# A hedgehog-attention and token-shift-MLP block: value products of the first three tiles in column halves, and a new order of the lists

## The chip, the cores and the metric

The kernel runs on one core of one Trainium2 chip. The metric is the device time of one execution in microseconds (us), the median of several runs. Engine names are those of the profile: PE is TensorE's matmul, PEld its weight load, DVE is VectorE, ACT is ScalarE, POOL is GpSimd, and SP is SyncE, which here only issues DMAs. A bank is one of the 8 banks of 2 KB per partition in PSUM, into which matmuls write.

## The reference

One block with two branches on x of 2048 tokens by 448 channels in bf16. H is 16 heads of 28 channels.

```
xn = layernorm(x)
# A: linear attention
q, k, v = split(xn @ wqkv)                      # 16 heads of 28
phi(u)  = [softmax(u @ w_phi), softmax(-(u @ w_phi))]
kv = phi(k)^T v ;  z = sum_s phi(k)
A  = (phi(q) kv / (phi(q) z + 1e-6)) @ wo
# B: token-shift MLP
h  = gelu(layernorm(xn) @ w1)                   # 448 -> 448
hs = four groups of 112 channels, shifted by +1, -1, +2, -2 tokens, @ w2
x1 = xn + hs
B  = x1 + gelu(layernorm(x1) @ w3) @ w4         # 448 -> 1792 -> 448
y  = x + A + B
```

## The kernel before

The tokens are 16 tiles of 128. Everything stays in SBUF: `xtok` (x), `xn` (normalized), `xnT` (its transpose, channels on partitions), `vaug` (the values with a column of ones per head), `phik` (features of the keys), `g_tok`/`gT` (the normalized x1 and its transpose), `hT` (the output of the first MLP).

**Two row halves.** A product over 448 channels is split into matmuls that use 64 rows of the PE array each. The lower and the upper 64 rows work at the same time, each into a bank of its own, so each product comes as a pair of lists. A value product of one tile (`z_v`, called ZV in the head's list) is 7 matmuls of 448 columns with the tile's `xnT` as weights and `wv` as the moving operand; a product with w1 (ZW) is 7 matmuls of 512 columns, and ZH is half of one, 7 matmuls of 256 columns. Transposes on TensorE (XT: `xn_T`, evacuated by `xn_out`) are 8 matmuls of 64x64 by an identity for each tile.

**Recorder.** All instructions are recorded in program order, and each engine executes its own in that order; semaphores are worked out from what they read and write. The line numbers in the profile are mostly those of the recorder's helpers: L204 is every matmul, L208 every transpose on TensorE, L212 an ACT instruction, L216 an elementwise instruction of DVE or POOL, L222 a DMA, L219 a DMA transpose. L737 is the product of the features of the keys with their normalizer on POOL.

**The loads** are issued by SP and ACT at the start, in the order in which they stand (`load_x(i, n)` loads n tiles from tile i, `load_half` half of a weight).

**The head** is a list given to `chain`. Its entries are executed in order. L entries are steps of the layernorm: "m" is statistics of a tile on DVE (bn_stats and bn_aggr), "q" its reciprocal root on ACT, "r" the same on POOL, "a" the application on DVE, "p" on POOL, "s" and "t" the statistics and root of tile 1 on ACT. XT are transposes, XD transposes by DMA, HD matmuls on constants that keep TensorE busy, FO the folding of `w_phi` into the weights of q and k, ZR the last 64 columns of the products with w1, HF the first pairs of the stage that follows. EV and EW are the evacuations of a value product and of a w1 product. "zip" jobs are interleaved between the two row halves by `chain` with a lag of 400 columns and a string of digits that says which half gets the next job first. `vb` and `gb` name the banks of the value products and of the w1 products.

**The rest** is a list given to `play`, executed in order. k0/k1 and q0/q1 are the products and exponentials of the key and query features, w0/w1_ the products with w2, kn and kx the normalizers and the products (POOL, L737) of the key features, lo and sc the statistics of the second layernorm, A and AD its application on POOL and DVE into `g_tok`, G its transpose by DMA into `gT` (issued by SP), K the products kv of a tile (matmuls of 64 columns on `phik` and `vaug`), a and b the products with w3 (512 columns on `gT`) and w4's input, T the transpose of the query features, N, f and S the output with its divisions and stores. `load_w4(h)` loads one of the two halves of w4, 784 KB, on SP; SP issues its DMAs in the list's order, and a DMA that waits for its data holds back all behind it.

Of the kernel before, what the change touches and what calls it, by code (L numbers as in the profile page):

```python
# [224 lines left out]
def bass_parallel_sum__linear_kernel_hedgehog__mixer_s_mlp__prompt_kernel(  # L225
    nc, A_x, A_wqkv, A_w_phi, A_wo, B_x, B_w1, B_w2, B_w3, B_w4, out,
):
    _, S, D = A_x.shape
# [14 lines left out]
    with es:  # L243
# [106 lines left out]
        def load_x(i, n, eng="SP"):  # L350
            R.dma(xtok[:, i:i + n, :], x2d[128 * i:128 * (i + n), :].rearrange("(j p) d -> p j d", p=128), eng)
# [9 lines left out]
        def load_half(dst, src, h, eng="SP"):  # L361
            R.dma(dst[:, 2 * h:2 * h + 2, :], src[192 * h:192 * h + 256, :].rearrange("(c p) d -> p c d", p=128), eng)
# [568 lines left out]
        def ZW(g, m, *then):  # L931
            return "zip", z_w1(g, m, gb[g][m]), then
# [21 lines left out]
        def HF(p, n):  # L954
# [4 lines left out]
        vb = {0: 5, 1: 6, 2: 5, 3: 0, 4: 7, 5: 5, 6: 0, 7: 1, 8: 0, 9: 6, 10: 3, 11: 2, 12: 7, 13: 7, 14: 5, 15: 2}  # L959
        gb = ((4, 2, 3), (7, 6, 4), (5, 0, 7), (0, 5, 6))  # L960
        spin(30)
        chain([
            L(("m", 0)), L(("s", 1, 0)), L(("q", 0, 1)), L(("s", 1, 1)), L(("a", 0)), HD(3, 3), L(("t", 1)), HD(0, 3),
            HD(1, 3), L(("p", 1)), L(("m", 2)), HD(5, 3), L(("q", 2, 1)), L(("m", 3)), do(load_w2, 0), HD(0, 3),
            HD(0, 3), XT(0, 5, 1, "2"), L(("m", 4)), L(("p", 2)), L(("q", 3, 1)), XT(1, 0, 1, "ACT"),
            ZV(0, EV(0, "ACT", 1)), XT(2, 0, 1, "ACT"), ZV(1, EV(1, "ACT", 1)), L(("q", 4, 1)), L(("m", 5)),
            L(("a", 4)), L(("p", 3)), ZH(2, 0), L(("q", 5, 1)), inside(1, ZH(1, 0), XT(3, 0, 1, "ACT")), L(("m", 7)),
            L(("q", 7, 1)), L(("m", 6)), L(("a", 7)), do(load_wT, 0, (1, 2, 3)), ZV(2, EV(2, "ACT", 1)),
            inside(1, ZH(0, 0), XT(4, 0, 1, "ACT")), L(("p", 5)),
            inside(2, ZH(0, 1, EW(0, 0, 1)), XT(5, 6, 1, "DVE")), L(("q", 6, 1)), L(("p", 6)), L(("m", 14)),  # L970
            L(("m", 15)), inside(1, ZH(2, 1), XT(7, 0, 1, "ACT")), ZV(4, EV(4, "ACT", 1)),
            inside(2, ZH(1, 1, EW(0, 1, 2)), XT(6, 0, 1, "DVE")), ZV(5, EV(5, "ACT", 1)), L(("r", 14, 1)),
            L(("r", 15, 1)), ZV(6, EV(6, "ACT", 1)), L(("m", 13)), ZW(1, 1, EW(1, 1, 1)), ZW(1, 2, EW(1, 2, 1)),
            L(("a", 14)), L(("a", 15)), L(("m", 12)), L(("m", 10)), XT(14, 1, 2, "2"), L(("r", 12, 1)),
            ZW(1, 0, EW(1, 0, 1)), L(("m", 11)), L(("m", 8)), L(("p", 12)), ZV(3, EV(3, "ACT", 1)), L(("r", 13, 1)),
            L(("a", 13)), L(("r", 10, 1)), ZV(7, EV(7, "DVE", 1)), L(("r", 8, 1)), L(("p", 8)),
            ZV(15, EV(15, "ACT", 1)), L(("a", 10)), XT(12, 6, 1, "2"), XD(10), XT(13, 3, 1, "DVE"),
            ZV(14, EV(14, "ACT", 1)), ZV(12, EV(12, "ACT", 1)), do(phi_blocks), L(("m", 9)), ZW(3, 0, EW(3, 0, 1)),
            L(("r", 11, 1)), XT(8, 1, 1, "2"), FO(1, 0, 0), L(("p", 11)), L(("r", 9, 1)), L(("p", 9)),
            ZW(3, 2, EW(3, 2, 1)), XD(11), FO(1, 0, 1), FO(1, 2, 0), ZW(3, 1, EW(3, 1, 1)), FO(1, 2, 1),  # L980
            do(load_w2, 1), ZV(13, EV(13, "ACT", 1)), ZV(8, EV(8, "DVE", 1)),
            inside(3, ZR(0, 6, (rest_out, 0, 6), (rest_T, 0)), XT(9, 1, 1, "DVE")), FO(0, 0, 0), FO(0, 2, 0),
            do(h_shift, 0), ZW(2, 2, EW(2, 2, 1)), ZW(2, 1, EW(2, 1, 1)), FO(0, 0, 1), ZW(2, 0, EW(2, 0, 1)),
            do(late_3), FO(0, 2, 1), ZV(9, EV(9, "DVE", 1)), do(kv_picks), ZR(1, 7, (rest_out, 1, 7)),
            ZV(10, EV(10, "DVE", 1)), ZV(11, EV(11, "DVE", 1)), HF(1, 0), HF(0, 0), HF(2, 0), do(load_w3, 0),
            do(kv_ones), do(h_shift, 1), do(rest_T, 1), HF(1, 1), HF(0, 1), HF(2, 1)], 400,
            "101001101001101000100110011110100")
# [62 lines left out]
        def wo_in(eng="SP"):  # L1050
# [1 line left out]

        K, G, S, T, kc, kb, W = kv_tile, g_T, store, q_T, kv_turn, kv_blocks, fin_tails
        play([
            (lo, 1), (load_w3, 1), (k0, 1), (w0, 2), (lo, 0), (kn, 0), (k1, 1), (q0, 1), (w1_, 2), (q1, 1), (T, 0),
            (k0, 2), (q0, 2), (k1, 2), (q1, 2), (k0, 3), (q0, 3), (T, 1), (kn, 1), (T, 3), (k1, 3), (w0, 4), (q1, 3),
            (kx, 0), (kn, 2), (T, 2), (kx, 1), (w1_, 4), (kn, 3), (k0, 4), (T, 5), (w0, 6), (k1, 4), (lo, 3), (kx, 2),
            (q0, 4), (lo, 2), (w1_, 6), (q1, 4), (kn, 4), (k0, 5), (kx, 3), (k0, 6), (sc, 0), (k1, 5), (w0, 8),
            (wo_in,), (q0, 5), (A, 0), (w1_, 8), (k1, 6), (T, 6), (AD, 1), (T, 4), (q0, 6), (kn, 5), (T, 7), (q1, 5),
            (w0, 10), (load_w4, 0), (A, 3), (k0, 7), (A, 2), (w1_, 10), (q1, 6), (lo, 5), (lo, 6), (w0, 12), (k1, 7),  # L1060
            (q0, 7), (G, 0), (K, 0), (kx, 4), (K, 1), (G, 1), (kx, 5), (lo, 7), (lo, 4), (G, 2), (K, 3), (K, 4),
            (G, 3), (sc, 4), (K, 6), (A, 7), (kn, 6), (K, 9), (q1, 7), (load_w4, 1), (A, 6), (A, 4), (w1_, 12),
            (K, 8), (K, 5), (K, 7), (lo, 10), (A, 5), (K, 11), (K, 2), (kx, 6), (G, 4), (kn, 7), (G, 7), (K, 10),
            (a, 0), (lo, 11), (kx, 7), (a, 1), (G, 6), (b, 0), (lo, 12), (b, 1), (w0, 14), (a, 2), (lo, 8), (a, 3),
            (lo, 9), (b, 2), (G, 5), (b, 3), (sc, 8), (w1_, 14), (T, 15), (a, 4), (a, 5), (b, 4), (b, 5), (T, 12),
            (lo, 14), (K, 13), (lo, 15), (T, 10), (K, 15), (K, 14), (T, 14), (K, 12), (a, 6), (a, 7), (A, 9), (b, 6),
            (G, 9), (b, 7), (kc,), (kb,), (T, 9), (A, 11), (AD, 10), (N, 1), (T, 11), (f, 1, 0), (N, 0), (a, 9),
            (AD, 8), (a, 8), (b, 9), (b, 8), (G, 10), (N, 2), (f, 2, 0), (a, 10), (G, 11), (lo, 13), (sc, 12),
            (A, 15), (a, 11), (N, 3), (b, 10), (G, 8), (f, 3, 0), (AD, 13), (A, 14), (b, 11), (f, 4, 0), (N, 5),
            (T, 13), (T, 8), (a, 12), (a, 13), (b, 12), (f, 1, 1), (b, 13), (S, 1), (A, 12), (N, 4), (f, 2, 1),  # L1070
            (N, 7), (a, 14), (f, 3, 1), (a, 15), (f, 4, 1), (b, 14), (G, 12), (S, 2), (b, 15), (S, 0), (N, 9),
            (G, 15), (f, 1, 2), (a, 16), (a, 17), (N, 6), (b, 16), (b, 17), (f, 2, 2), (G, 13), (N, 8), (a, 18),
            (f, 3, 2), (b, 18), (f, 4, 2), (a, 19), (N, 11), (a, 20), (G, 14), (S, 3), (f, 1, 3), (f, 3, 3), (N, 13),
            (b, 20), (b, 19), (f, 2, 3), (S, 5), (f, 4, 3), (a, 21), (N, 10), (a, 22), (S, 7), (b, 21), (f, 1, 4),
            (f, 3, 4), (S, 4), (b, 22), (N, 15), (f, 2, 4), (a, 23), (f, 4, 4), (S, 6), (a, 24), (b, 23), (f, 1, 5),
            (N, 12), (b, 24), (f, 2, 5), (N, 14), (a, 25), (S, 9), (S, 8), (f, 3, 5), (b, 25), (f, 4, 5), (a, 26),
            (a, 27), (b, 26), (b, 27), (f, 1, 6), (S, 10), (f, 2, 6), (fin_tails,), (f, 3, 6), (S, 12), (S, 13),
            (S, 11)])
        fin_full(14)
        fin_out(14)  # L1080
        store(14)
# [31 lines left out]
```

## Time and profile before

| | |
|---|---|
| median of 3 runs | 170.38 us (170.35 to 171.14) |
| the profiled execution's own time | 171.91 us |
| its span | 170.2 us |
| granted TensorE clock | 1.00 |
| PE busy | 164.4 us, 97% of the span, 2355 matmuls |
| DVE, POOL, ACT busy | 110.2, 91.0, 80.1 us |
| DMA | 19.93 MB, mean 117 GB/s |

A matmul's row gives its partitions and the columns that it streams ("64*128 64x448": 64 rows of weights 128 wide, 448 columns). "Busy" is the time in which the engine ran at least one of the instructions of a group, so overlapping matmuls count once, and the mean of one is longer than busy time over count. The chain of waits lists what the end of the execution hung on, piece by piece; "issue" in it is time in which an engine waited for nothing that the profile shows. In the table of DMA queues, "instruction" marks packets that carry instructions to the engines.

### The profile page before, as it was taken

To read this page: it belongs to the slowest core of one execution; us is meant where nothing else is said; L and a number is where in the kernel's file an instruction comes from. 1 tells how busy PE (TensorE), PEld (TensorE's weight loads), DVE (VectorE), ACT (ScalarE), POOL (GpSimd) and SP (SyncE) were. 2 spreads that over 40 slices of the span, in tenths; PEclk is the share of its full clock that TensorE was granted. 3 is DMA by queue.
4 is the path that set the end of the run, shared out by engine and by line. 5 is a ranking of instruction groups with operands and counts; after the bars stand their busy time and mean duration, and the time that the engine had idled before them with its cause. 6 is when DMAs were issued, how large, how long until landed. Compare 5 with 4: busy or idle time off the path is not lost.

```text
span 170.2 us, 5418 instructions
## 1 busy us (share of the span) xinstructions
PE 164.4 (97%) x2355; PEld 100.7 (59%) x2355; DVE 110.2 (65%) x249; ACT 80.1 (47%) x110; POOL 91.0 (53%) x124
## 2 busy tenths in 40 slices
PE   8699999999999999899999999999999999999994
PEld 7476778766888875444555455545555555545453
DVE  3679975669999999993785836745754252570031
ACT  4689775649998787445342430430240222224000
POOL 5633994002999999994365693162362634252040
PEclk9999999999999999999999999999999999999999
DMA  4996544988999966549885149363233112014021
GB/s 123 339 230 107 135 94 105 180 211 246 194 132 239 231 97 192 62 90 134 170 99 105 34 98 181 64 117 52 43 66 85 32 57 62 0 31 113 3 81 54
DMA packets 50553, 19.93 MB, mean 117 GB/s; under 512 B 41698, under 2 KB 49826, under 8 KB 50530
## 3 DMA queue, kind: packets, MB, share of 16 engines
q1 hardware_dynamic: 49410, 18.71, 54.2%
q10 hardware_dynamic: 1120, 0.89, 1.6%
q8 instruction: 18, 0.29, 0.8%
q14 instruction: 5, 0.04, 0.1%
HBM read 7.14 MB, written 1.84 MB: 53 GB/s over the span
## 4 chain that ended last, share of the span: by engine, by line
PE 90%; DMA 5%; SPq 2%; DVE 1%; issue 1%
PE banks L204 89%; DMA xtok<-in_A_x_dram 5%; SPq L222 2%; DVE st L216 1%; PE banks L208 0%; DVE mv L216 0%; DVE xnT L216 0%; DVE vaug L216 0%
## 5 line engine op out<-in xcount | busy, mean ns | idle before, releaser
L212 ACT ACTIVATE phik<-banks 128x1024 bf16<-128x1024 f32 (+1 forms) x44 | 41.7, 988 | 64.1 <-PE banks L204 64.0
L204 PE MATMUL banks<-gT,w 64*128 64x512 bf16 x392 | 47.3, 376 | 0.6 <-issue 0.5
L216 DVE TENSOR_TENSOR vaug<-banks,vaug 128x464 f32<-128x464 f32 (+3 forms) x65 | 32.8, 514 | 20.6 <-PE banks L204 18.8
L204 PE MATMUL banks<-w,phik 64*128 64x448 bf16 (+3 forms) x434 | 45.2, 343 | 0.0
L216 POOL TENSOR_TENSOR xnT<-vaug 128x280 bf16<-128x280 f32 (+1 forms) x32 | 18.1, 587 | 35.9 <-DVE vaug L216 35.9
L204 PEld LDWEIGHTS banks<-w,phik 64*128 64x128 bf16 (+1 forms) x434 | 22.3, 94 | 19.5 <-issue 0.4
L737 POOL TENSOR_TENSOR phik<-phik,rks 128x1792 bf16<-128x1792 bf16 x8 | 25.6, 3211 | 14.7 <-DVE rks L216 14.7
L204 PE MATMUL banks<-wv,xnT 64*128 64x448 bf16 (+2 forms) x222 | 32.1, 346 | 0.9 <-DMA wv<-in_A_wqkv_dram 0.6
L204 PEld LDWEIGHTS banks<-gT,w 64*128 64x128 bf16 x392 | 18.3, 94 | 20.1 <-ACT phik L212 1.2
L216 POOL TENSOR_TENSOR vaug<-xn,xtok 128x448 f32<-128x448 bf16 x16 | 16.2, 1031 | 9.1 <-DVE vaug L216 9.1
L204 PEld LDWEIGHTS banks<-wv,xnT 64*128 64x128 bf16 (+1 forms) x222 | 14.1, 94 | 9.4 <-DVE xnT L216 0.9
L216 DVE RECIPROCAL vaug<-banks 128x16 f32<-128x16 f32 x16 | 4.1, 257 | 22.0 <-PE banks L204 22.0
L204 PE MATMUL banks<-xnT,w 64*128 64x512 bf16 (+1 forms) x105 | 16.6, 334 | 0.1
L216 DVE TENSOR_REDUCE ksum<-phik 128x64 f32<-128x1792 bf16 x8 | 16.0, 1997 | 0.2 <-ACT phik L212 0.2
L204 PE MATMUL banks<-wpk,xnT 64*128 64x448 bf16 x112 | 15.9, 349 | 0.0
L204 PE MATMUL banks<-wpq,xnT 64*128 64x448 bf16 x112 | 15.6, 349 | 0.0
L212 ACT ACTIVATE hi<-banks 128x896 bf16<-128x896 f32 x16 | 14.0, 939 | 1.1 <-PE banks L204 1.1
L204 PE MATMUL banks<-w,hT 64*128 64x448 bf16 x96 | 14.4, 349 | 0.0
L216 POOL TENSOR_SCALAR g_tok<-xn,rs 128x512 bf16<-128x512 bf16 x12 | 9.1, 770 | 3.2 <-DMA gT<-g_tok 2.9
L216 DVE BATCH_NORM_STATS2 st<-xtok 128x6 f32<-128x448 bf16 x15 | 9.1, 607 | 2.1 <-DMA xtok<-in_A_x_dram 2.0
L204 PEld LDWEIGHTS banks<-wpk,xnT 64*128 64x128 bf16 x112 | 9.1, 94 | 2.2 <-ACT phik L212 0.2
L216 DVE TENSOR_TENSOR xn<-banks,xn 128x512 bf16<-128x512 f32 (+1 forms) x16 | 8.9, 600 | 1.6 <-PE banks L204 1.6
(68 smaller groups left out, 168.8 us busy)
## 6 DMA issues: line engine op xcount, KB each, us to landing
w<-in_B_w_dram SPq DMA_DIRECT2D x2, 896.0 KB, 5.4
out_dram<-vaug SPq DMA_DIRECT2D x15, 112.0 KB, 1.9
w<-in_B_w_dram SPq DMA_DIRECT2D x2, 784.0 KB, 5.0
xtok<-in_A_x_dram SPq DMA_DIRECT2D x2, 448.0 KB, 7.8
wv<-in_A_wo_dram SPq DMA_DIRECT2D x2, 224.0 KB, 3.4
xtok<-in_A_x_dram SPq DMA_DIRECT2D x3, 112.0 KB, 2.5
xtok<-in_A_x_dram ACTq DMA_DIRECT2D x3, 112.0 KB, 2.8
w<-in_B_w_dram SPq DMA_DIRECT2D x1, 336.0 KB, 4.3
```

The costliest lines, as they stand in the source:

```text
L204: self.op("PE", lambda e: e.matmul(out, lhsT, rhs, start=start, stop=stop, skip_group_check=True), [out], [lhsT, rhs], tile=self._tile(lhsT))
L212: self.op("ACT", lambda e: e.activation(out, in_, func, **kw), [out], [in_] + aps)
L216: self.op(eng, lambda e: getattr(e, name)(out, *args, **kw), [out], aps)
L222: self.op(eng, lambda e: e.dma_start(out, in_), [out], [in_], dma=True)
L737: R.op(pool, lambda e: e.tensor_tensor(ph, ph, wide, op=ALU.mult), [ph], [ph, wide, *after])
```

## The change

- wv's two halves are loaded after x's tiles 0 to 2 and ahead of tile 3; the first half is issued by ACT and the second by SP (before: the first by SP, the second by ACT, after tiles 0 to 3).
- The 64 last rows of w2 are loaded into both partition halves by two DMAs of 64 rows each in place of one with a doubled source.
- Tile 0 is applied (LH) and transposed and evacuated (XH) in two halves.
- The value products of tiles 0 to 2 are cut into two column halves of 224 (HC), each in a bank of its own; the row halves cross over, so that the lower rows work on one column half while the upper rows work on the other, and then change sides. Each tile has 14 matmuls of 224 columns in place of 7 of 448, and one evacuation on ACT for both halves (EC).
- Banks, the head's list, its string of digits and the list for `play` are re-ordered throughout. Tiles 1 and 3 are applied by DVE instead of POOL, 14 by POOL instead of DVE; the load of w2's main part moves from the head's SP queue to behind the transposes of `xn`.

The core of the diff:

```diff
         load_x(0, 1)
         load_x(1, 1, "ACT")
         load_x(2, 1)
+        load_half(wv, wv_d, 0, "ACT")
+        load_half(wv, wv_d, 1)
         load_x(3, 1, "ACT")
-        load_half(wv, wv_d, 0)
-        load_half(wv, wv_d, 1, "ACT")
         load_x(4, 1)
...
             if h:
-                tail = B_w2[REST:D, :]
-                R.dma(w2[:, NH, :], bass.AP(tail.tensor, tail.offset, [[0, 2], *tail.ap]), eng)
+                for k in range(2):
+                    R.dma(w2[64 * k:64 * k + 64, NH, :], B_w2[REST:D, :], eng)
...
+        def XH(i, b, c, eng="ACT"):
+            d, a = (xnT[:, c:c + 2, 128 * i:128 * i + 128].rearrange("p c (h e) -> p c h e", h=2),
+                    xn_t(b)[:, :, 0:128].rearrange("p h (c e) -> p c h e", c=2))
+            sides = tuple([(xn_t(b)[:, h, 64 * k:64 * k + 64], xn[lo:hi, i, 128 * (c + k):128 * (c + k) + 128],
+                            ident[lo:hi, lo:hi], None) for k in range(2)] for h, (lo, hi) in enumerate((LO, HI)))
+            return "both", sides, ((R.act, d, a, ACT.Copy) if eng == "ACT" else (R.ew, dve, "tensor_copy", d, a),)
+
+        def LH(i, c):
+            return do(ln_apply, dve, xn[:, i, 256 * c:256 * c + 256], xtok[:, i, 192 * c:192 * c + 256], mv, rs, i)
...
+        def HC(i, n, *then):
+            v = lap_pair([banks[vb[i] + k][:, 0:D // 2] for k in range(2)],
+                         lambda k, kc, lo, hi: xnT[lo:hi, kc, 128 * i:128 * i + 128],
+                         lambda k, kc, lo, hi: wv[lo:hi, kc, D // 2 * k:D // 2 * k + D // 2], False)
+            return "both", halves_of(*v[n], n == 0), then
+
+        def EC(i):
+            vd = vaug[:, i, :].rearrange("p (b h e) -> p b h e", b=2, e=VP)[:, :, :, 0:DH]
+            vs = two(vb[i])[:, :, 0:D // 2].rearrange("p b (h e) -> p b h e", e=DH)
+            return R.act, vd, vs, ACT.Copy
...
-            L(("m", 0)), L(("s", 1, 0)), L(("q", 0, 1)), L(("s", 1, 1)), L(("a", 0)), HD(3, 3), L(("t", 1)), HD(0, 3),
-            HD(1, 3), L(("p", 1)), L(("m", 2)), HD(5, 3), L(("q", 2, 1)), L(("m", 3)), do(load_w2, 0), HD(0, 3),
-            HD(0, 3), XT(0, 5, 1, "2"), L(("m", 4)), L(("p", 2)), L(("q", 3, 1)), XT(1, 0, 1, "ACT"),
-            ZV(0, EV(0, "ACT", 1)), XT(2, 0, 1, "ACT"), ZV(1, EV(1, "ACT", 1)), L(("q", 4, 1)), L(("m", 5)),
...
-            inside(2, ZH(0, 1, EW(0, 0, 1)), XT(5, 6, 1, "DVE")), L(("q", 6, 1)), L(("p", 6)), L(("m", 14)),
-            L(("m", 15)), inside(1, ZH(2, 1), XT(7, 0, 1, "ACT")), ZV(4, EV(4, "ACT", 1)),
-            inside(2, ZH(1, 1, EW(0, 1, 2)), XT(6, 0, 1, "DVE")), ZV(5, EV(5, "ACT", 1)), L(("r", 14, 1)),
...
-            "101001101001101000100110011110100")
+            HD(2, 3), L(("s", 1, 0)), L(("m", 0)), L(("q", 0, 1)), L(("m", 2)), L(("s", 1, 1)), HD(0, 3), HD(3, 3),
+            HD(0, 3), L(("t", 1)), HD(0, 3), L(("q", 2, 1)), LH(0, 1), LH(0, 0), L(("a", 1)), HD(0, 3),
+            XH(0, 0, 0, "DVE"), XH(0, 2, 2, "ACT"), L(("m", 3)), XT(1, 4, 1, "ACT"), L(("m", 4)), HC(0, 0),
+            L(("p", 2)), L(("m", 5)), L(("q", 3, 1)), XT(2, 1, 1, "ACT"), L(("a", 3)), HC(1, 0), L(("r", 4, 1)),
+            HC(0, 1, EC(0)), HC(2, 0), L(("a", 4)), L(("q", 5, 1)), L(("m", 7)), L(("m", 6)), HC(1, 1, EC(1)),
+            HC(2, 1, EC(2)), ZH(2, 0), inside(1, ZH(1, 0), XT(3, 4, 1, "ACT")), L(("p", 5)), L(("q", 7, 1)),
+            L(("a", 7)), inside(1, ZH(0, 0), XT(4, 0, 1, "ACT")),
+            inside(2, ZH(0, 1, EW(0, 0, 1)), XT(5, 5, 1, "DVE")), L(("q", 6, 1)), L(("m", 14)), L(("p", 6)),
+            inside(1, ZH(2, 1), XT(7, 0, 1, "ACT")), L(("r", 14, 1)), L(("m", 15)), ZV(5, EV(5, "ACT", 1)),
+            inside(2, ZH(1, 1, EW(0, 1, 2)), XT(6, 0, 1, "DVE")), L(("m", 13)), L(("r", 15, 1)),
...
+            "101101001110000101010011110100")
...
-            (w0, 10), (load_w4, 0), (A, 3), (k0, 7), (A, 2), (w1_, 10), (q1, 6), (lo, 5), (lo, 6), (w0, 12), (k1, 7),
-            (q0, 7), (G, 0), (K, 0), (kx, 4), (K, 1), (G, 1), (kx, 5), (lo, 7), (lo, 4), (G, 2), (K, 3), (K, 4),
-            (G, 3), (sc, 4), (K, 6), (A, 7), (kn, 6), (K, 9), (q1, 7), (load_w4, 1), (A, 6), (A, 4), (w1_, 12),
-            (K, 8), (K, 5), (K, 7), (lo, 10), (A, 5), (K, 11), (K, 2), (kx, 6), (G, 4), (kn, 7), (G, 7), (K, 10),
-            (a, 0), (lo, 11), (kx, 7), (a, 1), (G, 6), (b, 0), (lo, 12), (b, 1), (w0, 14), (a, 2), (lo, 8), (a, 3),
...
+            (AD, 1), (kn, 5), (w1_, 10), (k0, 7), (load_w4, 0), (A, 3), (G, 0), (w0, 12), (k1, 7), (G, 3), (G, 1),
+            (kx, 4), (A, 2), (kx, 5), (q0, 7), (K, 0), (K, 5), (K, 6), (lo, 4), (lo, 6), (lo, 7), (lo, 11), (G, 2),
+            (K, 1), (lo, 5), (K, 4), (K, 8), (q1, 7), (w1_, 12), (load_w4, 1), (kn, 6), (sc, 4), (K, 9), (K, 2),
+            (K, 3), (A, 5), (AD, 4), (K, 11), (K, 7), (K, 10), (a, 0), (a, 1), (b, 0), (A, 6), (kn, 7), (b, 1),
+            (w0, 14), (a, 2), (G, 5), (a, 3), (lo, 9), (b, 2), (A, 7), (kx, 6), (lo, 8), (b, 3), (w1_, 14), (G, 6),
...
```

More of the change, by code (lines that the diff above doesn't have):

```diff
@@ new lines, in bass_parallel_sum__linear_kernel_hedgehog__mixer_s_mlp__prompt_kernel @@
+            HC(2, 1, EC(2)), ZH(2, 0), inside(1, ZH(1, 0), XT(3, 4, 1, "ACT")), L(("p", 5)), L(("q", 7, 1)),
[3 more added lines that the diff above has]
+            inside(2, ZH(1, 1, EW(0, 1, 2)), XT(6, 0, 1, "DVE")), L(("m", 13)), L(("r", 15, 1)),
+            ZV(4, EV(4, "ACT", 1)), L(("a", 15)), ZV(6, EV(6, "ACT", 1)), L(("p", 14)), L(("r", 13, 1)), L(("m", 11)),
@@ new lines, in bass_parallel_sum__linear_kernel_hedgehog__mixer_s_mlp__prompt_kernel @@
+            L(("m", 12)), ZW(1, 0, EW(1, 0, 1)), do(load_wT, 0, (1, 2, 3)), L(("r", 11, 1)), ZW(1, 1, EW(1, 1, 1)),
+            ZW(1, 2, EW(1, 2, 1)), L(("m", 10)), XT(14, 3, 2, "2"), L(("r", 12, 1)), L(("a", 13)), L(("r", 10, 1)),
+            L(("m", 8)), ZV(7, EV(7, "ACT", 1)), L(("p", 12)), L(("a", 10)), ZV(3, EV(3, "ACT", 1)), do(phi_blocks),
+            ZV(15, EV(15, "ACT", 1)), XT(12, 6, 1, "2"), L(("r", 8, 1)), XT(13, 3, 1, "2"), L(("m", 9)),
+            ZV(14, EV(14, "DVE", 1)), ZV(12, EV(12, "DVE", 1)), L(("p", 8)), L(("p", 11)), ZW(3, 0, EW(3, 0, 1)),
@@ new lines, in bass_parallel_sum__linear_kernel_hedgehog__mixer_s_mlp__prompt_kernel @@
+            XT(8, 1, 1, "ACT"), L(("r", 9, 1)), FO(1, 0, 0), ZW(3, 2, EW(3, 2, 1)), FO(1, 0, 1), do(load_w2, 1),
+            L(("p", 9)), FO(1, 2, 0), XD(10), ZW(3, 1, EW(3, 1, 1)), FO(1, 2, 1), ZV(13, EV(13, "ACT", 1)),
+            ZV(8, EV(8, "ACT", 1)), XD(11), inside(3, ZR(0, 6, (rest_out, 0, 6), (rest_T, 0)), XT(9, 1, 1, "DVE")),
+            FO(0, 0, 0), do(load_w2, 0), do(late_3), do(h_shift, 0), FO(0, 2, 0), ZW(2, 2, EW(2, 2, 1)),
+            ZW(2, 0, EW(2, 0, 1)), ZW(2, 1, EW(2, 1, 1)), FO(0, 2, 1), do(kv_ones), do(load_w3, 0), FO(0, 0, 1),
@@ L989, in bass_parallel_sum__linear_kernel_hedgehog__mixer_s_mlp__prompt_kernel @@
+            ZV(9, EV(9, "ACT", 1)), ZR(1, 7, (rest_out, 1, 7)), ZV(10, EV(10, "DVE", 1)), do(kv_picks),
+            ZV(11, EV(11, "DVE", 1)), HF(1, 0), HF(0, 0), HF(2, 0), do(rest_T, 1), HF(1, 1), do(h_shift, 1), HF(0, 1),
+            HF(2, 1)], 400,
+            "101101001110000101010011110100")
         kp = [phi_pair(wpk, 2 * n, kq[n][0]) for n in range(8)]
@@ L1065, in bass_parallel_sum__linear_kernel_hedgehog__mixer_s_mlp__prompt_kernel @@
[L1065 to L1069, printed above, removed]
@@ new lines, in bass_parallel_sum__linear_kernel_hedgehog__mixer_s_mlp__prompt_kernel @@
+            (f, 1, 2), (a, 16), (N, 6), (a, 17), (b, 16), (f, 3, 2), (b, 17), (a, 18), (N, 8), (G, 15), (f, 2, 2),
+            (b, 18), (f, 4, 2), (a, 19), (a, 20), (N, 11), (f, 1, 3), (b, 20), (f, 3, 3), (S, 4), (S, 2), (N, 10),
+            (b, 19), (f, 2, 3), (f, 4, 3), (a, 21), (a, 22), (N, 13), (f, 1, 4), (b, 21), (S, 5), (f, 3, 4), (S, 7),
+            (N, 12), (b, 22), (f, 2, 4), (a, 23), (f, 4, 4), (a, 24), (S, 6), (b, 23), (b, 24), (f, 1, 5), (N, 14),
+            (a, 25), (S, 9), (f, 2, 5), (b, 25), (N, 15), (f, 3, 5), (a, 26), (f, 4, 5), (a, 27), (b, 26), (b, 27),
```

48 lines of the change are left out of this document (15 added, 33 removed).

## Prediction

> **What bounds the kernel now.** I read the head of the page first, then the chain of waits, then busy time by stretches.
>
> ```profile
> span 170.2 us, 5418 instructions
> PE 164.4 (97%) x2355; PEld 100.7 (59%) x2355; DVE 110.2 (65%) x249; ACT 80.1 (47%) x110; POOL 91.0 (53%) x124
> PE 90%; DMA 5%; SPq 2%; DVE 1%; issue 1%
> ```
>
> TensorE is busy for 97% of the span and carries 90% of the chain; no other engine passes 65%. So only three things can move the time: fewer or cheaper matmuls, less idle time of TensorE, or more of it. The chain tells where its idle time lies, and the stretches tell how much each has:
>
> ```profile
> 4.65 8.20 DMA xtok<-in_A_x_dram
> ...
> 14.47 0.31 DVE xnT L216
> 14.77 0.05 issue
> 14.82 2.19 PE banks L204 x19
> ...
> 65.83 2.77 PE banks L204 x24
> 68.59 0.49 issue
> 69.08 98.76 PE banks L204 x1245
> ```
>
> ```profile
> 5.10:9.20 4.10, 2.40 (x44) 1.43 (x38) 2.77 (x8) 2.42 (x9) 2.62 (x5) 1.00 1.07 360
> 9.20:14.80 5.60, 5.32 (x101) 4.30 (x101) 4.57 (x14) 5.13 (x11) 2.74 (x6) 1.00 1.09 170
> 14.80:62.20 47.40, 47.38 (x677) 36.40 (x679) 40.32 (x76) 37.20 (x54) 29.91 (x30) 1.00 0.80 169
> 69.10:168.00 98.90, 98.73 (x1246) 50.94 (x1245) 53.71 (x136) 27.10 (x28) 46.71 (x60) 1.00 0.42 78
> ```
>
> The second column of a stretch is its length, the third TensorE's busy time. From 5.10 to 9.20 it works 2.40 of 4.10 us, up to 14.80 it lacks 0.28 us, and after that 0.02 us up to 62.20 and 0.17 us from 69.10 on. One stall is left outside the head: 0.49 us at 68.59, where TensorE waits for nothing that the profile shows ("issue").
>
> So there are two places to argue about: the head up to 14.8 us, on which all the visible effort of the change is spent, and the stall at 68.59, which the change moves without naming it.
>
> **The head.** Rows by operation and shape, up to 16 us (busy, mean ns of one | idle before):
>
> ```profile
> L204 PE MATMUL banks<-wv,xnT 64*128 64x448 bf16 x40 | 7.3, 350 | 0.9 <-DMA wv<-in_A_wqkv_dram 0.6 <-DVE xnT L216 0.3
> L204 PE MATMUL banks<-xnT,w 64*128 64x256 bf16 x42 | 5.1, 270 | 0.1
> L204 PE MATMUL banks<-xnT,w 64*128 64x512 bf16 x3 | 0.8, 376 | 0.0
> L212 ACT ACTIVATE vaug<-banks 128x448 bf16<-128x448 f32 x4 | 2.2, 540 | 0.2 <-PE banks L204 0.2
> L216 DVE TENSOR_SCALAR xn<-xtok,mv,rs 128x512 bf16<-128x512 bf16 x5 | 1.8, 386 | 0.3 <-ACT rs L212 0.3
> L216 POOL TENSOR_SCALAR xn<-xtok,rs 128x512 bf16<-128x512 bf16 x5 | 3.8, 767 | 2.8 <-ACT rs L212 2.4
> L216 DVE COPY xnT<-banks 128x256 bf16<-128x256 bf16 x1 | 0.2, 249 | 0.0
> ```
>
> *The matmuls.* The value products of tiles 0 to 2 become 42 matmuls of 224 columns in place of 21 of 448: the same columns. From 512 to 256 columns the mean falls from 376 to 270 ns, 0.41 ns a column, so a matmul costs its columns and a fixed latency that overlaps the next one. I take 0 for the split. A latency that didn't overlap at all is excluded: 42 matmuls of 270 ns take 5.1 us and not 11.3. The dearest reading of the rows is 5.1 / 42 = 0.121 us for 256 columns against half of the 0.115 us that 512 columns cost further on (24 in 2.77 us, the row at 65.83): 21 x 0.064 = 1.3 us, less than the idle time of the stretch in which they run.
>
> The Trainium skill, TensorEngine Tiling (Array Packing), "Performance Considerations" under "Instruction Overhead", says that each matmul has about 60 cycles of overhead on TRN2; read at one column a cycle and 0.41 ns a column that is an estimate of 21 x 60 x 0.41 ns = 0.5 us against this change, in a stretch with idle time to take it; no row here shows 224 columns.
>
> *What it wins.* With both halves of wv loaded behind three tiles, tiles 0 to 2 can do all their value products while w1 is still on the way; before, 0.6 us of waiting for wv and part of 1.7 us (4.10 - 2.40) of other idle time in that stretch stood there. So TensorE is ahead by some 1 us at 9 to 10 us, at most 1.7.
>
> *What takes it back.* The transposed tile 6, `xnT`, is copied by DVE from 14.47 to 14.77, and TensorE goes on at 14.82. DVE reaches that copy only after the statistics of tiles 14 and 15:
>
> ```profile
> 12.88 0.63 DVE L216 BATCH_NORM_STATS2 st<-xtok 128x6 f32<-128x448 bf16 x1 [0.61 <-DMA xtok<-in_A_x_dram]
> ```
>
> They wait for rows 12 to 15 of x, issued by SP at 4.65 and landed 8.20 us later, at 12.85. The new list still has m14, m15 and then the copy of tile 6 on DVE, and SP still issues this load eighth, behind seven loads of the same sizes (wv's other half stands in the place of the first). Ahead of that copy stand the same products in both lists, so whatever TensorE wins before 14.8 it waits away there. The head is worth 0. Its bounds: DVE gets the applies of tiles 1 and 3 from POOL (2 x 0.386 = 0.77 us) and tile 0's in two pieces (0.1 us more, from 2 x 0.249 - 0.386); 0.61 us of idle time ahead of the statistics covers most of it, so at worst +0.3. POOL's 767 ns for each leaves it. If x lands sooner with the new order on ACT's queue, at best the same 0.61 us less wait, of which the products behind it pass on perhaps half: -0.3. ACT's copy of the two column halves stays one 128x448 instruction (540 ns), so it costs no more. The load of w2's main part leaves SP's head for a place before the first h shift; the transposes behind it come about 0.6 us sooner, and TensorE, which lacks 0.02 us in the whole stretch to 62.2, can't gain from it.
>
> *The rest of the lists.* The orders after the head can gain only what little idle time the stretches show and something at the end of the chain. I take -0.25 up to 65.8 (the 0.28 us that the second stretch lacks is the nearest row) and -0.2 behind 69.1 (its 0.17 us and a shorter end); bounds -0.6 and +0.3 for both, the latter if a copy between two products comes late.
>
> **The stall.** What does TensorE wait for at 68.59? Its instructions are loaded by a DMA queue of their own:
>
> ```profile
> q8 instruction: 18, 0.29, 0.8%
> ```
>
> 18 packets in 0.29 MB are 16 KB each, for 2 x 2355 matmuls and weight loads: one packet for 131 matmuls. It is small and regular, so I looked at which stretches had one. These are the rows of that queue in 60.4 to 61.5 and in 66.5 to 68; from 61.5 to 66.5 the view has only the last row, q1:
>
> ```profile
> q8 instruction: 1, 0.02, 5.2%
> ...
> q8 instruction: 1, 0.02, 4.7%
> ...
> q1 hardware_dynamic: 1446, 0.86, 71.9%
> ```
>
> Counted back from 68.59 over 131 matmuls (24, 96, 6 and 6 in the rows below) TensorE is at about 63.6, and there the next packet after the one near 61 is due; it comes only after 66.5. In between stands a load of w4 (784 KB) that SP issues at 62.55:
>
> ```profile
> 59.67 2.84 SPq L219 DMA_TRANSPOSE gT<-g_tok  x2
> 62.55 0.58 SPq L222 DMA_DIRECT2D w<-in_B_w_dram  x1
> ```
>
> The packet got through as that load ended, and TensorE, out of instructions, stood until 69.08. Now the change: it adds 21 matmuls (and 21 weight loads) to TensorE's stream ahead of this place, so the end of the block comes 21 matmuls earlier in the work. The rows around it:
>
> ```profile
> 62.64 0.95 PE L204 MATMUL banks<-phik,vaug 128*30 128x64 bf16 x96
> 63.53 0.74 PE L204 MATMUL banks<-wpq,xnT 64*128 64x448 bf16 x6
> 64.11 0.73 PE L204 MATMUL banks<-w,hT 64*128 64x448 bf16 x6
> 64.77 0.95 PE L204 MATMUL banks<-phik,vaug 128*30 128x64 bf16 x96
> 65.83 2.77 PE L204 MATMUL banks<-gT,w 64*128 64x512 bf16 x24
> ```
>
> The new list has the same five groups here in the same order. TensorE then stops not behind 24 of the 512-column matmuls (2.77 us, 0.115 each) but behind 3 of them, 2.4 us sooner; the point 131 matmuls ahead, where the next packet falls due, moves back by 21 of the quick ones (0.95 / 96 = 0.01 us each), 0.2 us. TensorE runs out 2.4 us earlier and the packet comes hardly earlier, so it needn't be faster or slower than before for the stall to grow.
>
> When does the packet come? If it still waits behind w4's load, that load's place decides. POOL:
>
> ```profile
> 56.32 2.29 POOL L216 TENSOR_SCALAR g_tok<-xn,rs 128x512 bf16<-128x512 bf16 x3
> 58.59 6.38 POOL L737 TENSOR_TENSOR phik<-phik,rks 128x1792 bf16<-128x1792 bf16 x2
> ```
>
> The new list puts only two applies ahead of the first of these products and the third behind it, and the last transposes before w4's load wait for that third one: 56.32 + 2 x 0.76 + 3.19 + 0.76 = 61.8, one transpose issue (2.84 / 2 = 1.42) to 63.2, against 62.55: w4 is 0.65 us later, and so is the packet and TensorE's restart, 69.7. Then 21 matmuls x 0.115 = 2.4 us more are still to do than before at its restart. The 0.25 us won before is waited away too. Sum: 0 (head) + 0.65 + 2.4 - 0.2 (order behind 69.1) = +2.85 us. The profiled execution took 171.91 us with a span of 170.2; the median of the runs is 170.38, and I carry the difference over one for one: 170.38 + 2.85 = 173.2 us.
>
> **The rivals.**
>
> *Ahead of the load (faster).* The packet falls due at about 63.2 (0.2 and 0.25 sooner than 63.6), and w4 is issued at 63.2 instead of 62.55, so this packet can get in first; in before it was due about 1 us behind the issue. It decides who is first in the DMA queues, and for this case speaks that the gap shrinks to zero. Landed by 65.5, it takes the stall away: -0.49, -0.25 and -0.2 of the orders: 169.4, with the head's bounds 169.1 to 169.8; say 169.5. The Trainium skill, Runtime: NRT & Kernel Launch, "Instruction fetch mechanics", has the sequencer fetch 16 KiB blocks on a DMA queue of its own, the crossing being "mostly hidden"; by that rule this case would hold, though the trace shows 0.49 us that were not hidden.
>
> *In between (no change).* The packet gets in first but late, or between the load's packets: from 69.08 - 66.5, TensorE restarts up to 2.6 us after the packet's start. Started at 64 to 64.5 it restarts at 66.5 to 67, where before it did its third such matmul at 66.2: +0.3 to +0.8 us, less 0.2 of the order behind it: 170.5 to 171.0, with the head's bounds 170.2 to 171.3; say 170.6.
>
> *The head is not pinned.* x lands sooner or DVE is late: -0.3 to +0.3 on any of these, already in the bounds. *The new pieces cost time.* If the 1.3 us above fell where TensorE doesn't wait: 171.7 without the larger stall. The idle 1.7 us speaks against it.
>
> **How the numbers follow.** The forecast gets 0.46: the rows show a packet held back by this very load, and the place where TensorE runs out lies 2.4 us earlier by count. Its own range is 172.3 to 173.8. Ahead of the load: 0.22, since due and issue times meet within some tenths that I can't resolve. In between: 0.26. The remaining 0.06 goes to the new pieces' cost. About 0.5%, 0.85 us, is what a measurement of this kernel can tell from no change: faster 0.22, same 0.26, slower 0.52. The range reaches from the faster case to the forecast's upper end, 169.4 to 173.8.
>
> **What would show it.** In the profile after: a row "issue" of 3 to 4 us on TensorE in the groups around 65.8, right behind the first 3 or so 512-column matmuls (right), or none there (the packet was ahead of w4's load). No q8 row in the stretch from about 62 to 66.5 says the packet was held. The head is right if TensorE waits up to 1 us for `xnT` at 14.8 and restarts at 14.5 to 15.1; earlier than 14.4 and the pin was wrong. The value matmuls of 224 columns should have a mean near 257 ns. A stall elsewhere on TensorE by more than 0.5 us would refute the sum.

## The result and the profile after

| | before | changed |
|---|---|---|
| median of 10 runs each, same session | 170.71 us (170.31 to 171.14) | 171.90 us (171.56 to 173.66) |
| ratio | | 1.0069, 95% interval 1.0041 to 1.0097 |
| a later session | 171.06 us (29 runs) | 171.99 us (12 runs), 1.0039 (1.0009 to 1.0069) |
| profiled execution: own time, span | 171.91, 170.2 us | 171.56, 169.8 us |

The changed kernel is slower in both sessions, by 0.7% and by 0.4%, about 1 us. Its profiled execution is nevertheless shorter than the one of before that the prediction was read from. Both facts have to come out of one account, and they do: the first row of the table is about medians, and the profiled execution of before was one of its late ones.

The page of the changed kernel, the lines that answer to those of before:

```profile
span 169.8 us, 5459 instructions
PE 165.5 (97%) x2376; PEld 102.5 (60%) x2376; DVE 111.3 (66%) x252; ACT 80.8 (48%) x111; POOL 89.2 (53%) x121
```

The chain of waits of the changed kernel (start, us, what):

```profile
4.31 7.85 DMA xtok<-in_A_x_dram
...
13.77 0.31 DVE xnT L216
...
14.12 2.83 PE banks L204 x25
...
65.28 0.59 PE banks L204 x3
65.87 0.54 issue
66.41 101.13 PE banks L204 x1265
```

The chain has the same shape as before. The head still ends with the copy of tile 6 behind the load of rows 12 to 15 of x, and the one stall of TensorE is still an "issue" among the 512-column matmuls. It now stands behind 3 of them instead of 24, as the count of instructions said, and is 0.54 us, not the 3 to 4 us of the forecast. The view of the DMA queues from 61.5 to 66.5 us, which had no packet of instructions before, now has one, and that is the prediction's own sign that the packet was not held:

```profile
q8 instruction: 1, 0.02, 1.9%
```

Busy time by stretches of the changed kernel (length, then TensorE, its weight loads, DVE, ACT, POOL; granted clock, DMA share, GB/s), and the two forms of the value products in its first 16 us:

```profile
5.10:9.20 4.10, 3.70 (x88) 3.08 (x83) 3.56 (x11) 2.71 (x9) 1.65 (x3) 1.00 1.03 338
9.20:14.80 5.60, 5.47 (x106) 4.00 (x101) 5.04 (x16) 5.13 (x12) 3.49 (x8) 1.00 1.05 178
14.80:62.20 47.40, 47.40 (x710) 36.71 (x707) 39.16 (x73) 38.66 (x56) 31.12 (x30) 1.00 0.82 168
```

```profile
L204 PE MATMUL banks<-wv,xnT 64*128 64x448 bf16 x21 | 3.5, 350 | 0.1
L204 PE MATMUL banks<-wv,xnT 64*128 64x224 bf16 x42 | 2.7, 257 | 0.4 <-DVE xnT L216 0.2 <-DMA wv<-in_A_wqkv_dram 0.2
```

In these two profiles TensorE works 3.70 us from 5.10 to 9.20 instead of 2.40. Most of that difference is the late head of the first profile. Over the five profiles with the old head as it is TensorE works 3.2 us in this stretch on average (2.40 to 3.57), over eight with the new head 3.6 us (2.89 to 4.00), so the change wins about 0.4 us here. The 42 short matmuls have a mean of 257 ns and cost 0.064 us each.

### The profile page after: what moved, and what is told of

It reads as the page before. It is cut to its first block, busy times and chain, and to the rows that moved or that the text cites. A ratio compares the mean times of both kernels' runs of the same rounds, so it can differ in the third digit from the quotient of the medians.

```text
span 169.8 us, 5459 instructions
## 1 busy us (share of the span) xinstructions
PE 165.5 (97%) x2376; PEld 102.5 (60%) x2376; DVE 111.3 (66%) x252; ACT 80.8 (48%) x111; POOL 89.2 (53%) x121
## 4 chain that ended last, share of the span: by engine, by line
PE 90%; DMA 5%; SPq 2%; DVE 1%; issue 1%
PE banks L204 89%; DMA xtok<-in_A_x_dram 5%; SPq L222 2%; DVE st L216 1%; PE banks L208 0%; DVE mv L216 0%; DVE xnT L216 0%; DVE vaug L216 0%
## 5 line engine op out<-in xcount | busy, mean ns | idle before, releaser
L204 PEld LDWEIGHTS banks<-gT,w 64*128 64x128 bf16 x392 | 18.8, 94 | 20.7 <-ACT phik L212 1.8
L204 PE MATMUL banks<-wv,xnT 64*128 64x448 bf16 (+3 forms) x243 | 30.7, 330 | 0.5 <-DVE xnT L216 0.2
L204 PE MATMUL banks<-xnT,w 64*128 64x512 bf16 (+1 forms) x105 | 15.9, 334 | 0.0
L216 POOL TENSOR_TENSOR rs<-mv,mhalf 128x1 f32<-128x1 f32 (+1 forms) x13 | 9.1, 699 | 3.9 <-DVE mv L216 3.8
L204 PEld LDWEIGHTS banks<-wpq,xnT 64*128 64x128 bf16 x112 | 8.7, 94 | 2.1 <-ACT phik L212 0.2
```

The source lines that it names most:

```text
L204: self.op("PE", lambda e: e.matmul(out, lhsT, rhs, start=start, stop=stop, skip_group_check=True), [out], [lhsT, rhs], tile=self._tile(lhsT))
L216: self.op(eng, lambda e: getattr(e, name)(out, *args, **kw), [out], aps)
```

## The experiments

Two theories. A block is what one packet of the instruction queue brings. **Instruction fetch:** 21 more matmuls ahead make TensorE's block of instructions end sooner in the work, where the next packet of instructions has not come yet. **Head and orders:** the loss comes from the new head or the new lists. All runs of a kernel here vary by about 2 us, and the kernel before, run as a kernel of its own, came out at 1.0037 (0.9997 to 1.0077) of itself; a ratio within 0.4% of 1 is not read by itself below, and the profiles decide.

### 21 matmuls more, 21 fewer

The kernel before with the length of its blocks moved as in the changed kernel, and the changed kernel with it moved back. The constant matmuls at the start stream nearly the same columns in both (3840 against 3825 and 3843), and `turns` is a constant as wide as the matmul. Only the lines that matter are shown.

```diff
-                R.mm(banks[7][:, 0:128], busy, busy, True, True)    # spin(30)
+                R.mm(banks[7][:, 0:75], busy, turns, True, True)    # before, spin(51)
+                R.mm(banks[7][:, 0:427], busy, turns, True, True)   # changed, spin(9)
```

> The kernel before with 21 more matmuls at its start and nothing else: its 30 constant matmuls of 128 columns become 51 of 75 (3840 against 3825 columns). Theory 1 (instruction fetch: the 21 added matmuls end TensorE's block of instructions behind 3 instead of 24 of the 512-column matmuls near 66 us): slower than before by 0.8 to 3 us, with the idle time "issue" behind the third such matmul. Theory 2 (the loss comes from the new head and the new orders): within 0.3 us of before.

> The changed kernel with 21 fewer matmuls at its start and nothing else: its 30 constant matmuls of 128 columns become 9 of 427 (3840 against 3843 columns), so the blocks of TensorE's instructions end where they did before. Theory 1 (instruction fetch): faster than the changed kernel by 1 to 2 us, so 170 to 171 and at or below the kernel before, with the idle time back behind 24 matmuls or gone. Theory 2 (head and orders): stays at 171.9, within 0.3 us.

Measured: before with 51 constant matmuls 172.56 us beside before's 171.09, ratio 1.0083 (1.0050 to 1.0115). The changed kernel with 9: 171.43 us, 1.0014 (0.9982 to 1.0045) of before. TensorE's 512-column matmuls in the timelines, first of before with 51, then of the changed kernel with 9:

```profile
65.57 0.59 PE L204 MATMUL banks<-gT,w 64*128 64x512 bf16 x3
66.97 2.96 PE L204 MATMUL banks<-gT,w 64*128 64x512 bf16 x25 [0.81 <-issue]
```

```profile
65.49 3.38 PE L204 MATMUL banks<-gT,w 64*128 64x512 bf16 x28
```

The stall and the loss came to the kernel before with 21 small matmuls more at its start. The stall left the changed kernel with as many taken away, and its ratio is not told apart from 1; the median fell by 0.5 us from the 171.90 of the first session, where 1 to 2 us had been expected. Nothing of the new head or lists is needed for it. Without a stall the 28 matmuls run as one row.

### The load of w4 moved

```diff
-            (K, 1), (lo, 5), (K, 4), (K, 8), (q1, 7), (w1_, 12), (load_w4, 1), (kn, 6), ...
+            ... (w0, 14), (a, 2), (G, 5), (load_w4, 1), (a, 3), ...     # later
+            ... (lo, 11), (load_w4, 1), (G, 2), (K, 1), ...             # earlier
```

> The changed kernel with the second load of w4 behind one more transpose of g_tok on SP's queue, so some us later and out of the way of the packet. Theory 1 (the packet of instructions waits behind that load in part of the executions): faster than the changed kernel by 0.5 to 1.5 us, the idle time at 66 us 0.6 us or less in every execution and the runs closer together. Theory 2: within 0.3 us of 171.9.

> The changed kernel with the second load of w4 one transpose earlier on SP's queue, by some 1.4 us, so ahead of the packet always. Theory 1: the packet comes when that load ends, about 65.5 to 66 us, TensorE restarts at 67.5 to 68.5 instead of 66.4: slower than the changed kernel's best executions by 1 to 2 us, 172 to 173.5. Theory 2: within 0.3 us of 171.9.

> The changed kernel with 9 constant matmuls of 427 columns for 30 of 128 (blocks of TensorE's instructions end where they did before) and the second load of w4 one transpose later on SP. Theory 1 (packet of instructions, held by that load or not): no idle time behind the 512-column matmuls in any execution, so the runs' spread shrinks to about 1 us and the median falls to 170.3 to 171.0, as fast as the best runs with either edit alone or faster. Theory 2 (the spread and the loss come from the head's loads): 171.4, with the spread of the 9-matmul kernel (170.3 to 172.6).

> The kernel before with the second load of w4 one transpose later on SP, nothing else. Theory 1: its slower executions, those with idle time behind 24 matmuls, go: 0.3 to 0.6 us faster in the median than before, spread 1 us or less. Theory 2: within 0.2 us of before with the same spread of some 2 us.

In the kernel before, the load went behind its `(G, 4)`. Measured with the load later: changed kernel 171.92 us, 1.0051 (1.0020 to 1.0082); changed with 9 constant matmuls 171.09 us, 1.0009 (0.9980 to 1.0039); before 170.58 us, 0.9995 (0.9964 to 1.0026). The spreads stayed (170.5 to 172.2 and 169.7 to 172.0 in the last two). The stall of the changed kernel with the load later:

```profile
65.74 0.59 PE L204 MATMUL banks<-gT,w 64*128 64x512 bf16 x3
67.00 2.98 PE L204 MATMUL banks<-gT,w 64*128 64x512 bf16 x25 [0.67 <-issue]
```

With no load of w4 near, the stall is still 0.67 us, against what both the prediction and this expectation assumed: the changed kernel stalls without the load. By the records of its own trace, the packet of the changed kernel starts at 63.47 us and the first data of the load move at 63.62, so the packet was ahead by 0.15 us. Nor does the stall make the spread of the runs.

The load earlier measured something else. The transpose of `gT` that the 512-column matmuls need was now behind the load and took 6.69 us to land, and TensorE waited for that; the ratio of 1.0149 (1.0084 to 1.0215) says nothing on the packet. Its chain (this execution took 177.95 us at a granted clock of 0.98, so the size of the wait is its own; the ratio rests on others of 173.09 to 174.57 us):

```profile
61.82 0.59 SPq L222
62.41 0.04 issue
62.45 6.69 DMA gT<-g_tok
```

This trace does show a packet that is held. The data of the load move from 63.07 to 66.44 us, and the packet, due 131 matmuls ahead of the block's end, at 63.1, starts at 66.67. The first profile of before has the same picture: data from 63.81 to 66.89, packet at 66.72. So the prediction read that profile rightly. In the five profiles where the load's data were first by 1 us or more, the packet started 1.8 to 3.6 us behind its due place, in all others 0.8 to 1.7; in the changed kernel the packet was first.

### The dose: 4 and 10 fewer, 32 more

The same edit as above with other numbers, on the changed kernel.

> The changed kernel with 26 constant matmuls of 148 columns for 30 of 128 at its start: 4 fewer. Theory 1, as the runs so far left it (the packet of instructions takes its time even when nothing is in its way, and TensorE's block ends too soon for it): the idle time "issue" moves from behind 3 to behind 7 of the 512-column matmuls and is 4 x 0.115 = 0.46 us shorter than the 0.5 to 0.8 us of the profiles so far, so 0.1 to 0.4 us; from the first of these matmuls to the end 104.1 to 104.4 us, between the 103.8 of the kernels without it and the 104.5 to 104.9 of those with it behind 3. A rival (a fixed cost of the block's end, or of these matmuls): the idle time stays 0.5 to 0.8 us, wherever it falls.

> The changed kernel with 20 constant matmuls of 192 columns for 30 of 128: 10 fewer, so TensorE's block ends behind 13 of the 512-column matmuls, 1.15 us of work later than in the changed kernel. If the idle time is what is left of the packet's own time (packet's end + 1.4 us, which fell 0.5 to 0.8 us too late so far): gone, or at most 0.2 us; from the first of these matmuls to the end 103.6 to 103.9 us. If it is a fixed cost of a block's end among these matmuls: 0.5 to 0.8 us behind 13, and 104.5 to 104.9 us to the end.

> The changed kernel with 62 constant matmuls of 62 columns for 30 of 128: 32 more, so the block ends 29 of the quick 64-column matmuls ahead of the first 512-column one, some 0.65 us earlier than in the changed kernel, while the packet falls due only some 0.3 us earlier. If the idle time is what is left of the packet's own time: 0.8 to 1.2 us, inside the quick matmuls, and slower than the changed kernel by 0.2 to 0.5 us. If it is a fixed cost: 0.5 to 0.8 us and the same time.

Measured: 4 fewer 171.52 us, 1.0040 (1.0009 to 1.0071); 10 fewer 170.91 us, 0.9962 (0.9922 to 1.0001); 32 more 173.16 us, 1.0101 (1.0054 to 1.0149). The timelines, in this order:

```profile
64.90 1.02 PE L204 MATMUL banks<-gT,w 64*128 64x512 bf16 x7
66.51 2.54 PE L204 MATMUL banks<-gT,w 64*128 64x512 bf16 x21 [0.58 <-issue]
```

```profile
66.08 3.20 PE L204 MATMUL banks<-gT,w 64*128 64x512 bf16 x28
```

```profile
65.96 0.72 PE L204 MATMUL banks<-phik,vaug 128*30 128x64 bf16 x68
67.99 0.39 PE L204 MATMUL banks<-phik,vaug 128*30 128x64 bf16 x28 [1.31 <-issue]
```

The place moves with the count each time: behind 7; nowhere; 28 quick matmuls ahead of the first 512-column one, where 29 were expected. The stall is 1.31 us for the earliest end and gone for the latest: it is what is left of the packet's own time, not a fixed cost. Two runs missed their expectations: with 4 fewer the stall was 0.58 us and not 0.1 to 0.4, with 32 more 1.31 and not 0.8 to 1.2. The trace's own records of the packets say why for the first. Times in us; "group" is the start of the first 96 quick matmuls, near which the packet falls due:

| kernel | group | packet starts | packet ends | TensorE runs out | restarts | restart after packet's end |
|---|---|---|---|---|---|---|
| before, first profile | 62.64 | 66.72 | 67.84 | 68.59 | 69.08 | 1.24 |
| changed | 61.93 | 63.47 | 64.98 | 65.87 | 66.41 | 1.43 |
| before with 51 | 62.38 | 64.05 | 65.52 | 66.16 | 66.97 | 1.45 |
| changed, w4 later | 62.40 | 64.66 | 65.62 | 66.33 | 67.00 | 1.38 |
| changed with 26 | 61.59 | 63.34 | 65.11 | 65.92 | 66.51 | 1.40 |
| changed, second profile | 62.30 | 63.88 | 65.57 | 66.24 | 66.81 | 1.24 |
| changed with 62 | 63.72 | 65.48 | 66.77 | 66.68 | 67.99 | 1.22 |
| before, second profile | 61.54 | 63.22 | 64.84 | (never) | | |

TensorE restarts 1.22 to 1.45 us after its packet has ended, whatever held it. With 26, the packet ended 3.52 us after the group's start, in the changed kernel 3.05: 0.47 us that ate the 0.46 us won by 4 matmuls. One execution can't show a dose of that size; 10 fewer could.

Counted from the program's first matmul, the stall stands behind 1109 matmuls in six of the seven profiles that have one, and behind 1110 in the seventh, whatever work the kernel does there. The place 131 matmuls ahead of it is where the prediction had the packet fall due. From there TensorE restarts after 3.9 to 4.2 us in six of the seven, and after 5.55 us in the first profile of before, where the load was in front. The 131 matmuls themselves take 2.6 us with 32 more, 3.3 in the changed kernel, 3.6 with 4 fewer, 4.2 with 10 fewer and 5.1 in the kernel before. The stall is what the first time exceeds the second by, and with 10 fewer or in the kernel before nothing is left of it, but for the first profile of before.

### Before once more

> The kernel before, unchanged, for a second profile of it: the first has a span of 170.2 us. If that execution was a typical one, the span is again within 0.3 us of it and TensorE again stands about 0.5 us behind 24 of the 512-column matmuls (the prediction took it for typical). If it was a late one of a wide spread, the span is 168.5 to 169.5 and the idle time there is less or none, the packet of instructions having come before 66 us.

The span was 168.5 us, and the 28 matmuls one row:

```profile
64.76 3.20 PE L204 MATMUL banks<-gT,w 64*128 64x512 bf16 x28
```

So the first profile was not a typical one: it has a stall that none of the 8 other profiles with the block's end behind 24 matmuls shows, and a late head. From the first 512-column matmul to the end of the span it took 170.2 - 65.83 = 104.37 us. In the changed kernel, profiled twice, it is 104.52 and 104.55, in the two others with the stall behind 3 (before with 51, w4 later) 104.93 and 104.66: 104.7 on average. In the second profile of before it is 103.74, and in all profiles without the stall 103.6 to 103.9. The stall behind 3 costs 0.9 us. That is more than its idle time, which starts only when the third matmul has run out (3 take 0.59 us with nothing behind them, and 0.34 in the stream). The medians differ by 0.9 us in the later session and by 1.2 in the first, where the interval leaves 0.7 to 1.7, so the stall is enough for the loss.

### The heads and the lists

> The head of the kernel before with the changed kernel's list for what follows the head: it has the old number of matmuls, so blocks of instructions end where they did. If the new order of the later list is worth what the prediction took (-0.25 to -0.45 us), 170.2 to 170.6 beside before's 170.7 to 171.1; if the new order costs (the rival to instruction fetch alone), 0.3 us or more above before.

> The kernel before with the statistics of tiles 14 and 15 on DVE behind the copy of tile 6 instead of ahead of it. If that copy's wait for rows 12 to 15 of x holds the head (the prediction's pin): no wait of TensorE for DVE's xnT near 14.8 us, 0.2 to 0.5 us faster in the median than before and its slow executions, those with a late load, closer to the fast ones. If the transposes of tile 14, which need the same rows, come late instead: within 0.2 us, with the wait some us later in TensorE.

> The changed kernel with 9 constant matmuls of 427 columns and the statistics of tiles 14 and 15 behind the copy of tile 6. If the new head's gain is given back at that copy (the prediction's reason for a head worth 0): 0.5 to 1 us faster than with the 9 matmuls alone, so 170.4 to 170.9 and faster than before. If it is given back later anyway: 171.1 to 171.5, no faster than before.

> The kernel before with rows 12 to 15 of x loaded by ACT's queue right behind w1's second half (issue at about 3.2 us) instead of last on SP's (4.2 to 4.65 us); nothing else. If the landing of these rows sets when the head ends, and with it the spread of the runs: landing at 10.5 to 11.5 instead of 11.7 to 13.4, no wait for DVE's xnT at 14.8, 0.3 to 0.6 us faster in the median than before and fewer runs above 171.3. If the issue on ACT (0.5 to 0.9 us, ahead of the sums of tile 1) delays the first value products more than that: 0.2 to 0.6 us slower.

The edits: before's head with the changed `play` list; the two statistics behind the copy (in the changed kernel with tile 14's root behind them),

```diff
-  ..., L(("m", 14)), L(("m", 15)), inside(1, ZH(2, 1), ...), ..., inside(2, ZH(1, 1, ...), XT(6, 0, 1, "DVE")), ...
+  ..., inside(1, ZH(2, 1), ...), ..., inside(2, ZH(1, 1, ...), XT(6, 0, 1, "DVE")), L(("m", 14)), L(("m", 15)), ...
```

and `load_x(12, 4, "ACT")` ahead of `load_x(6, 2)`.

Measured: before with the new list 170.76 us, 0.9990 (0.9954 to 1.0025): the new order of the list neither gains the 0.25 to 0.45 us of the prediction nor loses as much. Statistics behind the copy: before 172.44 us, 1.0088 (1.0056 to 1.0120), slower where a gain or no change had been expected; changed with 9 matmuls 171.43 us, 1.0036 (1.0005 to 1.0066), no better than without. The pin can't simply be taken out; the chain of before with that edit shows what is late next:

```profile
13.37 0.42 DVE xnT L216
13.80 0.54 DVE st L216
...
19.99 0.30 DVE xn L216
...
20.34 0.29 PE banks L208 x8
```

DVE goes from the copy into a chain of statistics and applies that ends at the transposes of tile 14 at 20.3 us, for which TensorE waits 0.33 us; at 27.5 it stands 0.52 us more, for nothing that the profile shows. This is part of the 1.5 us that the edit costs, and the rest stays open. With rows 12 to 15 on ACT's queue: 170.83 us, 0.9976 (0.9942 to 1.0010), not told apart from none; in its profile these rows land at 11.38 us and rows 8 to 11 in turn at 13.28.

When TensorE starts its first 512-column matmul tells what head and list are worth, stall aside: 64.76 to 65.83 us in five profiles with the old head (mean 65.4), 64.90 to 66.51 in eight with the new one (65.6). The spread has its counterpart in the loads: rows 12 to 15 land between 10.77 and 13.43 us in these profiles, and the latest start (66.51) belongs to the latest landing. With the old head the five starts come in the order of the landings. With the new head they don't: the earliest landing, 10.77, has a start of 65.49, so the loads alone don't set it.

### Side by side

> The changed kernel, unchanged, beside the next two on the same chip: 0.4 to 1.0% slower than before, 0.5 to 0.8 us of idle time behind the third 512-column matmul, 104.5 to 104.9 us from the first of them to the end.

> The changed kernel with 20 constant matmuls of 192 columns for 30 of 128, once more with more rounds: 0.7 to 1.1 us faster than the changed kernel beside it (no idle time at the block's end), and level with before, 0.995 to 1.002. If the 0.9962 of its first run was more than noise, below before by 0.3 to 0.8 us.

> The same with rows 12 to 15 of x loaded by ACT's queue behind w1's second half. If the landing of these rows sets the spread: 0.2 to 0.5 us faster in the median than with 20 constant matmuls alone and the fastest kernel here, 0.990 to 0.997 of before; if ACT's time ahead of tile 1 counts: no better than that one.

Measured on one chip, with before at 171.06 us: changed 171.99 us, 1.0039 (1.0009 to 1.0069); with 20 constant matmuls 170.87, 0.9985 (0.9948 to 1.0023); with those and rows 12 to 15 on ACT 170.92, 0.9973 (0.9936 to 1.0011). The changed kernel again:

```profile
65.65 0.59 PE L204 MATMUL banks<-gT,w 64*128 64x512 bf16 x3 [0.15 <-issue]
66.81 2.98 PE L204 MATMUL banks<-gT,w 64*128 64x512 bf16 x25 [0.56 <-issue]
```

Moving the block's end by 10 matmuls takes 1.1 us off the changed kernel's median and makes it level with before. No version here is faster than before beyond the intervals; the best ratios are 0.996 to 0.998.

## Why the prediction was right and wrong

- **Right: the block's end.** The prediction derived from a count of packets that TensorE would stop behind 3 instead of 24 matmuls, and it does; moving the count alone moves the stall and the loss. The direction, slower, follows from it.
- **Wrong step: "When does the packet come? If it still waits behind w4's load".** In the changed kernel it doesn't. The load was issued at 62.36 us and not at 63.2 (the working from POOL's rows was 0.8 us late), but the packet fell due 0.7 us earlier too, at 62.5, and started at 63.47, 0.15 us ahead of the load's first data. So the term 0.65 + 2.4 us was mis-sized: what it measured is 0.9 us, with a restart at 66.41 us, not 69.7, and an idle time of 0.54 to 0.81 us behind 3 matmuls, not 3 to 4.
- **Right mechanism under a rival's name, wrong price.** The rival "in between" gave a restart at 66.5 to 67; 66.41 to 67.00 was measured. It was priced at +0.1 to +0.6 us, a restart 0.3 to 0.8 us behind the place of the third matmul, less 0.2 for the new order. In their own timelines the four profiles with the stall behind 3 restart 0.8 to 1.1 us behind that place (66.41 - 65.28 - 3 x 0.115 = 0.79 in the changed kernel), and the 0.2 was not seen. The price is 0.9 us, above the 0.85 us that the prediction took as the bound of no change.
- **Wrong step: the base.** "I carry the difference over one for one" took the profiled execution of before as typical. Its own time of 171.91 us beside a median of 170.38 was the sign: in nearly every later run own time and span differ by about 1.75 us, so a median of 170.38 is a span of 168.6, not of 170.2. This is not what made the forecast too high: against an execution without a stall, a restart at 69.7 us would have cost 0.5 us more.
- **Right in the mean, open in the price: the short matmuls at 0.** The mean is 257 ns, as forecast from the other shapes. They cost 2.7 us for 42, 0.064 us each. Beside the 448-column ones of the same stretch (3.5 us for 21) that is no loss; by the rate of 512 columns further on (0.115 us each, so 0.050 for 224) it is 0.6 us more. The estimate of 0.5 us from the Trainium skill, TensorEngine Tiling (Array Packing), "Instruction Overhead", is neither shown nor excluded by these rows.
- **Right in the sum, incomplete in the reason: the head at 0.** The forecast gain of some 1 us at 9 us is 1.3 us of work in the first two profiles, but 0.4 us over five and eight; at 66 us the two heads are level. In the changed kernel TensorE goes on behind the copy of tile 6 at 14.12 us, earlier than the 14.4 below which the prediction called its pin wrong. The path is the one it named, but rows 12 to 15 landed 0.7 us sooner than in the profile that it read (12.16 against 12.85 us). That this copy takes back what the head wins is not shown: with the statistics moved behind it, neither kernel became faster. The bounds of 0.3 us were too narrow for one execution: these loads alone spread by 2.7 us.
- **Not seen: -0.25 and -0.2 us of the lists.** The new list on the old head is at 0.9990 (0.9954 to 1.0025) and takes 103.87 us from the first 512-column matmul, the old one 103.74.
- **The rival "ahead of the load (faster)"** was half true: the packet did come ahead of the load, and still too late, as it ends 1.5 us after it starts and TensorE restarts 1.4 us behind that. The Trainium skill, Runtime: NRT & Kernel Launch, "Instruction fetch mechanics", calls the crossing mostly hidden; at this crossing 11 profiles agree and 7 show 0.49 to 1.31 us, so here it depends on how fast the 131 matmuls ahead of the crossing run, and once on the load.

## What to carry to other kernels

An added instruction costs more than its own time where it moves the end of a block of instructions behind a run of quick ones: here 131 matmuls, most of them of 64 columns, are used up in 3.3 us, and the next block needs 3.9 to 4.2. Look for "issue" idle time on the bounding engine, count instructions to the place, and move the count by a few (here 10 matmuls at the start, at no cost that these runs show) before judging an edit by its time. And compare the profiled execution's own time with the median before taking its stalls as typical.

## What the runs showed that was not expected

A packet of 16 KB of instructions took 0.9 to 2.0 us, and TensorE restarted 1.22 to 1.45 us after it had ended. The place of the stall could be set almost to the matmul from a count alone: behind 3, behind 7, and 28 quick matmuls ahead where 29 were counted. And the loads of the first 13 us landed up to 2.7 us apart over thirteen profiles. Between the two profiles of the kernel before, rows 12 to 15 land 1.2 us apart and the first 512-column matmul starts 1.1 us apart, of 1.7 us between their spans; that this makes the 2 us by which all runs of one kernel differ is likely, and not shown.
